# The last score block of a head pair as a step of its own, one MLP piece behind, in a fused attention and mixer kernel

## The chip, the core and the metric

The kernel runs on one core of one Trainium2 chip. The metric is the device time of one execution in microseconds (us), lower is better. Before the change it is 579.77 us, the median of 3 runs (577.92 to 579.84).

A core has the engines PE (matrix products, written into PSUM), ACT (activation functions), DVE and POOL (elementwise work and reductions), and SP, which here only issues DMA transfers. PEld is PE's loading of weights, beside its matmuls. PSUM has 8 banks for each partition, each of 512 fp32 columns.

## The reference

Attention with RMS-normalised queries and keys, then a mixer block on its output:

```python
q: (8 batches, 12 heads, 448 tokens, 64)      # k and v alike
q_n, k_n = rmsnorm(q, g_q), rmsnorm(k, g_k)
attn = softmax(q_n @ k_n.T / sqrt(64))
x = (attn @ v), heads side by side            # (8, 448, 768)
u = x + (x.T @ U @ V).T                       # U (448, 32), V (32, 448): along the tokens
out = u + relu(u @ w_ch1) @ w_ch2             # w_ch1 (768, 3072), w_ch2 (3072, 768)
```

## The kernel before

**Pieces of work.** For each batch the MLP is cut into 24 *up* pieces (`up`, L681: six matmuls of 448 columns into one PSUM tile `ph`, then one relu on ACT) and 24 or 32 *down* pieces (`down`, L728: six matmuls of 384 columns). Four down pieces in a row add into one PSUM tile `po`, which is allocated at part 0 and read by DVE (L738) after part 3. Between them stand the mixer's steps `mix_t` and `mix_two` for the next batch, whose results go through DMA transposes into `uT`.

Attention goes by pairs of heads, six pairs to a batch, two to a group (24 groups of four heads). The 448 keys of a pair of heads are three blocks of 128 for each head and a last stretch of 64 for each; the two stretches of 64 form one block together, the *last block*. In the loop `Spair` (from group 6 on) scores one pair: two blocks into two one-bank tiles `sl` (L455), their exponentials (ACT, L457), four blocks into two tiles `sc` of two banks each (L464), the last block into a third `sl` (L466), its exponential (L467), and the two exponentials of the `sc` tiles (L469). `Vall` (L529, L533) multiplies the exponentials of the pair before with the values.

The last 64 queries of a group are worked apart: `rest_tile` allocates a tile `pr`, `rest_products` (L560) fills it for both pairs of the group before, `rest_norms` (DVE) divides it into `x_rest` (the tile that traces call `xr`). `Spair` gets that group's number as `rest` where it does this work first: at the first pair of a group, except where a separate step `Rest` does it (first pair of batches 2 and 3). `Srows` is the form of the step in batch 1.

**PSUM.** The pool `ps_sc` has two buffers of two banks, the pool `ps` four of one bank. All of `ph`, `po`, `pv`, `pr`, `sl` and the mixer's small tiles come from `ps`; a new tile waits until the last reader of the buffer it gets is done.

**Order.** Instructions run in the order in which the program issues them on each engine. Batch 0's attention is written out by hand (`FRONT`). The rest is merged from two lists, `att` (attention steps with a cost) and `mlp` (MLP pieces with a cost). At each turn an attention step is taken if the sum of attention costs so far is at most `due` of the sum of MLP costs, and if `ready` allows it; otherwise an MLP piece is. `at` holds an estimate of when PE, ACT and DVE are done with what has been issued, and `runs` adds to it. `after_pair` is true from a `Spair` to the next MLP piece. If a mixer step comes next while it is true, a down piece from behind is moved ahead of it. An MLP piece of a batch whose attention is not complete waits (`done_at`, `may_mlp`).

**Other steps named below.** `squares`, `sums`, `roots` and `scale_all` prepare queries and keys of later groups (POOL L144, ACT L141, DVE L167, ACT L174 and L175, POOL L179, L198 and L202), `turn_dma` and `take_dma` turn them by DMA (L391, L393) and scale `qT` on POOL (L399), `load` fetches later groups, `weights` issues the loads of `w_ch1` and `w_ch2` from POOL's queue (L295, L303).

Of the kernel before, what the change touches and what calls it, by code (L numbers as in the profile page):

```python
# [12 lines left out]
AF = mybir.ActivationFunctionType  # L13
# [14 lines left out]
def kernel(  # L28
# [13 lines left out]
    nc = tc.nc  # L42
    B, H, S, D = q.shape
# [6 lines left out]
    NJ = S // P  # L50
    SM = NJ * P
    R = S - SM
# [7 lines left out]
    NPAIR = H // 2  # L60
    HALF = dm // 2
    scal = 1.0 / (D ** 0.5)
# [65 lines left out]
    def load(gi):  # L128
        stage_tiles(gi)
        for i in range(2):  # L130
            load_qk(gi, i)
        load_v(gi)
# [138 lines left out]
    bias = gg[:, 1:2]  # L271
# [79 lines left out]
    at = {"pe": 0.0, "act": 0.0, "dve": 0.0}  # L351
    exp_done = {}

    def runs(eng, us):
        at[eng] = us + (at["pe"] if eng == "pe" else max(at["pe"], at[eng]))

    qk, es, xs = {}, {}, {}
# [87 lines left out]
    def Spair(b, pr, rest=None):  # L445
        qT, kT = qk[divmod(b * NPAIR + pr, 2)]
        E = es[(b, pr)] = ep.tile([P, NB, S], BF16, name="E", tag="E")
        ts = [ps.tile([P, 512], FP32, name="sl", tag="ps")[:, :S] for _ in range(2)]
        if rest is not None:
            rest_tile(rest)  # L450
            rest_products(rest)
            rest_norms(rest)
        for i in range(2):
            d = slice(i * D, (i + 1) * D)
            nc.tensor.matmul(ts[i], kT[d, 2 * P:3 * P], qT[d], start=True, stop=True)  # L455
        for i in range(2):
            nc.scalar.activation(E[:, 4 + i, :], ts[i], AF.Exp, scale=scal, bias=bias)  # L457
        runs("pe", 0.4)
        runs("act", 1.04)
        tiles = [ps_sc.tile([P, 2, 512], FP32, name="sc", tag="sc") for _ in range(2)]  # L460
        for r in range(2):
            for i in range(2):
                d = slice(i * D, (i + 1) * D)
                nc.tensor.matmul(tiles[r][:, i, :S], kT[d, r * P:(r + 1) * P], qT[d], start=True, stop=True)  # L464
        last = ps.tile([P, 512], FP32, name="sl", tag="ps")[:, :S]
        nc.tensor.matmul(last, kT[:, SM:], qT, start=True, stop=True)  # L466
        nc.scalar.activation(E[:, 6, :], last, AF.Exp, scale=scal, bias=bias)  # L467
        for r in range(2):
            nc.scalar.activation(E[:, 2 * r:2 * r + 2, :], tiles[r][:, :, :S], AF.Exp, scale=scal, bias=bias)  # L469
        runs("pe", 0.6)  # L470
        runs("act", 2.3)
        exp_done[(b, pr)] = at["act"]

    def Srows(blocks, rest=None):
# [43 lines left out]
    x_rest = [consts.tile([P, dm], BF16, name=f"xr{i}") for i in range(2)]  # L518
# [48 lines left out]
    def rest_norms(gi):  # L567
        b, h0, _ = groups[gi]
        pv = rest_tiles.pop(gi)
        lo, hi = (0, R) if b % 2 else (R, P)  # L570
        r = headp.tile([P, 2], FP32, name="r", tag="r")
        nc.vector.reciprocal(r, pv[:, :, D])
        for e in range(2):
            rows = slice(e * R, (e + 1) * R)
            c = (h0 + 2 * e) * D
            nc.vector.tensor_tensor(
                x_rest[b % 2][lo:hi, c:c + 2 * D].rearrange("p (h d) -> p h d", d=D),
                pv[rows, :, :D],
                r[rows].rearrange("p h -> p h ()").to_broadcast([R, 2, D]), ALU.mult)
        runs("dve", 0.6)  # L580

    def rest_tile(gi):
        rest_tiles[gi] = ps.tile([P, 2, D1], FP32, name="pr", tag="ps")
# [168 lines left out]
    def add_att(cost, f, *a):  # L752
        att.append((cost, f, a))
# [15 lines left out]
    for i, (b, pr) in enumerate(pairs):  # L769
        if b == 0:  # L770
            continue
        gi, a = divmod(i, 2)
        more = gi + 1 < len(groups)
        by_dma = gi + 1 >= DMA_FROM
        soon = gi + 2 < len(groups)

        rest = gi - 1 if a == 0 and (pr > 0 or b > APART) else None
        if a == 0 and pr == 0 and b > 1:
            add_att(0.8, Vall, *pairs[i - 1])
            if gi == DMA_FROM:  # L780
                add_att(0.0, sums, gi + 1, 0)
                add_att(0.0, sums, gi + 1, 1)
                add_att(0.0, scale_all, gi + 1)
            if b <= APART:
                add_att(0.5, Rest, gi - 1)
        if gi >= DMA_FROM:
            add_att((0.5 if a == 1 and soon else 1.0) + (0.35 if rest is not None else 0.0), Spair, b, pr, rest)
            if a == 0 and more:
                add_att(0.0, turn_dma, gi + 1)
                add_att(0.0, take_dma, gi + 1)  # L790
                if gi + 3 < len(groups):
                    add_att(0.0, load, gi + 3)
            if pr != 0:
                add_att(0.5, Vall, *pairs[i - 1])
                if a == 1 and soon:
                    add_att(0.0, squares, gi + 2, 0)
                    add_att(0.0, squares, gi + 2, 1)
                add_att(0.25, lambda: None)
                if a == 1 and soon:
                    add_att(0.0, sums, gi + 2, 0)  # L800
                    add_att(0.0, sums, gi + 2, 1)
                    add_att(0.5, lambda: None)
                    add_att(0.0, scale_all, gi + 2)
            continue

        if a == 0:
            add_att(0.45, Srows, ((b, pr, 0), (b, pr, 1)), rest)
            if pr == 0:
                add_att(0.8, lambda: None)
            if not by_dma:  # L810
                add_att(0.0, squares, gi + 1, 0, nc.gpsimd)
                add_att(0.0, squares, gi + 1, 1, nc.gpsimd)
                if gi + 2 < DMA_FROM:
                    add_att(0.0, load, gi + 3)
            if pr != 0:
                add_att(0.9, Vall, *pairs[i - 1])
            add_att(0.0, sums, gi + 1, 0)
            add_att(0.0, sums, gi + 1, 1)
            add_att(1.0, Srows, ((b, pr, 2), (b, pr + 1, 0), (b, pr, 3)))
            add_att(0.0, scale_all, gi + 1)  # L820
            if gi + 2 == DMA_FROM:
                add_att(0.0, squares, gi + 2, 0, nc.gpsimd)
                add_att(0.0, squares, gi + 2, 1, nc.gpsimd)
                add_att(0.0, weights, 2)
            add_att(0.4, lambda: None)
        else:
            add_att(0.6, Srows, ((b, pr, 1), (b, pr, 2), (b, pr, 3)))
            if gi + 2 == DMA_FROM:
                add_att(0.0, load, gi + 3)
            if not by_dma:  # L830
                add_att(0.5, Vall, *pairs[i - 1])
                add_att(0.39, T, gi + 1, 0)
                add_att(0.39, T, gi + 1, 1)
                continue
            add_att(0.0, squares, gi + 2, 0)
            add_att(0.0, squares, gi + 2, 1)
            add_att(0.5, Vall, *pairs[i - 1])
            add_att(0.0, turn_dma, gi + 1)
            add_att(0.0, take_dma, gi + 1)
            add_att(0.0, load, gi + 3)  # L840
# [5 lines left out]
    for n, (c, f, a) in enumerate(att):  # L846
        gi = a[0] if f is Rest else a[2] if f is Spair else None
# [5 lines left out]
    mlp = []  # L853
    for b in range(B):
# [14 lines left out]
        tiles = [(col, half) for col in cols for half in range(2)]  # L869
        if b == 0:  # L870
            tiles.sort(key=lambda t: t[1])
        if b == B - 1:
            tiles = tiles[:-2]
# [68 lines left out]
    for step in FRONT.split():  # L942
# [4 lines left out]
            fill_mixer()  # L947
        if name == "val":
            load(int(a[0]) + 3)
    for i in range(2):  # L950
        nc.gpsimd.memset(x_rest[i][R:] if i else x_rest[i][:R], 0.0)
    weights(2)

    at.update(pe=0.0, act=0.0, dve=0.0)
# [27 lines left out]

    def ready(f, a):
        if f is Spair:
            if a[2] is not None and mlp[im][1] is down and mlp[im][2][3] > 0:
                return False
            if im > 0 and mixes(mlp[im - 1][1]):
                return False
            return at["dve"] <= at["pe"] + 0.3 and at["act"] <= at["pe"] + 0.6
        if f in (Vall, Rest) and ca >= a_one and (after_pair or after_v):  # L990
            return False
        if f is sums and a[0] > DMA_FROM:
            return not any(m[1] is mix_t for m in mlp[max(0, im - 1):im + 3])
        if ca >= a_one:
            return True
        if f is Vall:
            return exp_done[a[:2]] <= at["pe"] + 0.1
        return f is not Srows or at["act"] <= at["pe"] + 0.6

    later, turning, after_pair, after_v = [], False, False, False  # L1000
    while ia < len(att) or im < len(mlp):
# [6 lines left out]
        if take_att:  # L1008
            c, f, a = att[ia]
# [4 lines left out]
            after_pair = after_pair or f is Spair  # L1014
# [8 lines left out]
        else:  # L1023
            f = mlp[im][1]
# [4 lines left out]
            after_pair = after_v = False  # L1029
            c, f, a, _ = mlp[im]  # L1030
# [34 lines left out]
```

## Time and profile before

| | |
|---|---|
| runs shown | 579.84, 577.92, 579.77 us |
| the profiled execution | 579.34 us, of which 577.6 us are its span |
| granted PE clock | 1.0 |
| busy share of the span | PE 98%, ACT 53%, POOL 36%, DVE 33% |
| matmuls | 4762 |
| DMA | 68.20 MB, mean 118 GB/s |

Times in the rows are microseconds from the start of the span. A row of the timeline has start, length, engine, line of the kernel and operation, output and inputs by their names in the program, the count of instructions that the row holds together, and in brackets the idle time before it with what ended it. Rows of the same kind in close succession are merged, so that rows of one engine can overlap. Matmuls are pipelined and their ends are modelled: what PE's queue really spends on a matmul is the distance from its start to the next start.

### The profile page before, as it was taken

The page shows a single profiled execution, that of the slowest core. Times are in us where ns is not written, and L with a number is a line of the kernel's source. Part 1 is how long each engine was busy: PE and PEld are TensorE (multiplying, and loading weights), DVE is VectorE, ACT ScalarE, POOL GpSimd, SP SyncE. Part 2 cuts the span into 40 slices and gives each one's busy share as a digit, 9 for nine tenths or more (in the row PEclk, how much of TensorE's full clock was granted, in tenths as well). Part 3 has the DMA queues.
Part 4 walks back from the last instruction along what each step waited for, and adds up shares of the span by engine and source line. Part 5 has one row for each costly group of instructions (what it writes and reads, how often), then busy time and mean ns, then how long its engine had stood idle before and what let it go on. Part 6 is the DMA issues. An engine that isn't in the chain of part 4 may idle for free.

```text
span 577.6 us, 11577 instructions
## 1 busy us (share of the span) xinstructions
PE 564.9 (98%) x4762; PEld 323.2 (56%) x4762; DVE 191.2 (33%) x426; ACT 308.3 (53%) x516; POOL 206.2 (36%) x308
## 2 busy tenths in 40 slices
PE   8899999999999999999999999999999999999997
PEld 7665555555655555555555555555565555555565
DVE  6865655312343221621234321631123410410011
ACT  5977760788453876367654478258744344014300
POOL 6874793365313615334514523342531000000000
PEclk9999999999999999999999999999999999999999
DMA  9999999784436742497246735275212310220022
GB/s 226 180 245 238 251 234 207 140 204 84 120 76 159 177 111 39 93 206 184 39 121 100 193 100 131 59 186 147 34 35 57 75 30 0 69 62 0 1 56 55
DMA packets 104829, 68.20 MB, mean 118 GB/s; under 512 B 66632, under 2 KB 100936, under 8 KB 104776
## 3 DMA queue, kind: packets, MB, share of 16 engines
q1 hardware_dynamic: 95124, 57.83, 43.4%
q0 software_dynamic: 9408, 9.44, 9.8%
q8 instruction: 37, 0.61, 0.5%
q10 hardware_dynamic: 244, 0.20, 0.1%
q14 instruction: 16, 0.13, 0.1%
HBM read 52.20 MB, written 11.01 MB: 109 GB/s over the span
## 4 chain that ended last, share of the span: by engine, by line
PE 80%; DMA 9%; ACT 3%; POOL 3%; issue 3%; SPq 0%; DVE 0%; POOLq 0%; ACTq 0%
PE po L728 34%; PE ph L681 33%; DMA kf<-in_k_dram 6%; PE pv L533 3%; DMA w2b<-in_moe_w_ch_dram 3%; PE sl L455 2%; ACT E L457 2%; POOL sq L144 2%; ACT E L435 1%; PE sl L466 1%; PE po L715 1%; PE sc L464 1%; PE pr L560 1%; PE pv L529 1%; PE sc L614 1%
## 5 line engine op out<-in xcount | busy, mean ns | idle before, releaser
L681 PE MATMUL ph<-uT,w1b 128*128 128x448 bf16 x1128 | 223.1, 352 | 1.1 <-DMA uT<-u_rest 0.7
L728 PE MATMUL po<-w2b,hT 128*128 128x384 bf16 x1296 | 221.9, 326 | 1.1 <-DMA w2b<-in_moe_w_ch_dram 1.0
L728 PEld LDWEIGHTS <-hT 128*128 128x128 bf16 x1296 | 123.5, 98 | 84.8 <-issue 7.1
L681 PEld LDWEIGHTS <-w1b 128*128 128x128 bf16 x1128 | 108.5, 98 | 98.7 <-issue 3.8
L688 ACT ACTIVATE hT<-ph 128x448 bf16<-128x448 f32 x186 | 98.3, 550 | 110.1 <-PE ph L681 109.7
L457 ACT ACTIVATE E<-sl,gg 128x448 bf16<-128x448 f32 x72 | 41.6, 630 | 79.2 <-PE sl L455 78.1
L399 POOL TENSOR_SCALAR qT<-qT,gg 128x448 bf16<-128x448 bf16 x36 | 50.5, 1402 | 92.2 <-DMA qT<-qn 80.7
L198 POOL TENSOR_TENSOR qn<-qf,rs 128x384 bf16<-128x384 f32 x36 | 29.9, 829 | 116.6 <-ACT rs L175 109.8
L469 ACT ACTIVATE E<-sc,gg 128x896 bf16<-128x896 f32 x72 | 68.9, 1020 | 0.0
L738 DVE TENSOR_TENSOR ob<-po,x 128x384 f32<-128x384 f32 x46 | 25.6, 557 | 108.9 <-PE po L728 104.9
L167 DVE TENSOR_REDUCE ssq<-sq 128x14 f32<-128x896 f32 x45 | 47.1, 1079 | 27.6 <-ACT sq L141 25.0
L537 DVE RECIPROCAL r<-pv 128x6 f32<-128x6 f32 x42 | 8.2, 195 | 124.2 <-PE pv L533 123.9
L435 ACT ACTIVATE E<-sc,gg 128x896 bf16<-128x896 f32 (+1 forms) x42 | 37.0, 952 | 2.2 <-PE sc L430 2.0
L533 PE MATMUL pv<-va,E 128*128 128x65 bf16 x756 | 35.4, 194 | 0.0
L533 PEld LDWEIGHTS <-E 128*128 128x128 bf16 x756 | 32.4, 98 | 3.4
L198 POOL TENSOR_TENSOR kp<-kf,rs 128x384 bf16<-128x384 f32 x36 | 29.8, 828 | 0.0
L529 PE MATMUL pv<-vl,E 128*128 128x130 bf16 x126 | 27.6, 219 | 0.0
L621 DVE TENSOR_TENSOR x<-sc,x 128x384 bf16<-128x384 f32 x42 | 20.8, 550 | 17.6 <-PE sc L614 17.6
L174 ACT ACTIVATE rs<-ssq,eps 128x28 f32<-128x28 f32 (+1 forms) x24 | 7.5, 314 | 35.6 <-DVE ssq L167 35.5
L538 DVE TENSOR_TENSOR x<-pv,r 128x384 bf16<-128x384 f32 x42 | 23.4, 557 | 1.4
L467 ACT ACTIVATE E<-sl,gg 128x448 bf16<-128x448 f32 x36 | 22.9, 637 | 0.0
L206 POOL CAST va<-vf 128x768 bf16<-128x768 f32 x24 | 20.7, 861 | 1.2 <-DMA vf<-in_v_dram 1.2
(123 smaller groups left out, 429.9 us busy)
## 6 DMA issues: line engine op xcount, KB each, us to landing
qf<-in_q_dram SPq DMA_DIRECT2D x23, 448.0 KB, 3.8
kf<-in_k_dram SPq DMA_DIRECT2D x23, 448.0 KB, 5.2
vf<-in_v_dram SPq DMA_DIRECT2D x48, 192.0 KB, 6.0
out_dram<-ob SPq DMA_DIRECT2D x48, 192.0 KB, 2.7
w2b<-in_moe_w_ch_dram POOLq DMA_DIRECT2D x8, 576.0 KB, 16.8
w1b<-in_moe_w_ch_dram POOLq DMA_DIRECT2D x2, 1152.0 KB, 19.2
vf<-in_v_dram SPq DMA_DIRECT2D x48, 32.0 KB, 5.2
w1b<-in_moe_w_ch_dram POOLq DMA_DIRECT2D x1, 1536.0 KB, 29.4
```

Source lines behind the costliest of these rows:

```text
L167: nc.vector.tensor_reduce(ssqs[gi][:, i, :], sqs.pop((gi, i)), AX, ALU.add)
L198: nc.gpsimd.tensor_tensor(main.rearrange("p (t i) d -> p i t d", i=2), src[:, c, :2 * NJ].rearrange("p (i t) d -> p i t d", i=2), rs[:, c, ...
L399: nc.gpsimd.tensor_scalar(qT[:, a], qT[:, a], gg[:, 0:1], None, ALU.mult)
L435: nc.scalar.activation(es[(b, pr)][:, 2 * r:2 * r + n, :], sc[:, :n, :S], AF.Exp, scale=scal, bias=bias)
L457: nc.scalar.activation(E[:, 4 + i, :], ts[i], AF.Exp, scale=scal, bias=bias)
L469: nc.scalar.activation(E[:, 2 * r:2 * r + 2, :], tiles[r][:, :, :S], AF.Exp, scale=scal, bias=bias)
L529: nc.tensor.matmul(pv[:, i].rearrange("p e d -> p (e d)"), E[:, 2 * NJ, w:w + P], vl[:, lp, :], start=True, stop=False)
L533: nc.tensor.matmul(pv[:, i, e, :], E[:, 2 * j + e, w:w + P], va[:, (lp + 2 * e) * NJ + j, :], start=False, stop=(e == 1 and j == NJ - 1))
L681: nc.tensor.matmul(ph, w1b[:, dt, ht * P:(ht + 1) * P], uT[:, dt, off:off + S], start=(dt == 0), stop=(dt == KD - 1))
L688: nc.scalar.activation(hT[:, ht, off:off + S], ph, AF.Relu)
L728: nc.tensor.matmul(po, hT[:, ht, col:col + P], w2b[:, ht, half * HALF:(half + 1) * HALF], start=(ht == 0), stop=(ht == KH - 1))
L738: nc.vector.tensor_tensor(ob[:, h], po, urows(b, col, half), ALU.add)
```

## The change

In a pair that carries a rest, `Spair` no longer scores the last block. A step `Slast` behind it does: its matmul and its exponential. `ready` holds `Slast` back until an MLP piece has been taken since the pair. The cost of the step, 1.35 with the rest, is charged at `Slast` instead of at `Spair`. In pairs without a rest `Spair` calls `Slast` itself, in the old place. The condition that kept a pair with a rest from being taken while a down product is open (next MLP piece a `down` with a part over 0) is dropped.

In `ready`, an `Srows` that carries a rest is now also held back while DVE's estimate is more than 0.9 ahead of PE's.

The two memsets of `x_rest` on POOL move from the end of the written-out part, ahead of two weight loads, into the list of attention steps, behind the squares for group 4 in group 3.

```diff
--- before.py
+++ after.py
@@ -462,13 +462,21 @@
             for i in range(2):
                 d = slice(i * D, (i + 1) * D)
                 nc.tensor.matmul(tiles[r][:, i, :S], kT[d, r * P:(r + 1) * P], qT[d], start=True, stop=True)
+        if rest is None:
+            Slast(b, pr)
+        for r in range(2):
+            nc.scalar.activation(E[:, 2 * r:2 * r + 2, :], tiles[r][:, :, :S], AF.Exp, scale=scal, bias=bias)
+        runs("pe", 0.4)
+        runs("act", 1.78)
+        exp_done[(b, pr)] = at["act"]
+
+    def Slast(b, pr):
+        qT, kT = qk[divmod(b * NPAIR + pr, 2)]
         last = ps.tile([P, 512], FP32, name="sl", tag="ps")[:, :S]
         nc.tensor.matmul(last, kT[:, SM:], qT, start=True, stop=True)
-        nc.scalar.activation(E[:, 6, :], last, AF.Exp, scale=scal, bias=bias)
-        for r in range(2):
-            nc.scalar.activation(E[:, 2 * r:2 * r + 2, :], tiles[r][:, :, :S], AF.Exp, scale=scal, bias=bias)
-        runs("pe", 0.6)
-        runs("act", 2.3)
+        nc.scalar.activation(es[(b, pr)][:, 2 * NJ, :], last, AF.Exp, scale=scal, bias=bias)
+        runs("pe", 0.2)
+        runs("act", 0.52)
         exp_done[(b, pr)] = at["act"]
 
     def Srows(blocks, rest=None):
@@ -579,6 +587,10 @@
                 r[rows].rearrange("p h -> p h ()").to_broadcast([R, 2, D]), ALU.mult)
         runs("dve", 0.6)
 
+    def fill_rest():
+        for i in range(2):
+            nc.gpsimd.memset(x_rest[i][R:] if i else x_rest[i][:R], 0.0)
+
     def rest_tile(gi):
         rest_tiles[gi] = ps.tile([P, 2, D1], FP32, name="pr", tag="ps")
 
@@ -784,7 +796,9 @@
             if b <= APART:
                 add_att(0.5, Rest, gi - 1)
         if gi >= DMA_FROM:
-            add_att((0.5 if a == 1 and soon else 1.0) + (0.35 if rest is not None else 0.0), Spair, b, pr, rest)
+            add_att(0.0 if rest is not None else 0.5 if a == 1 and soon else 1.0, Spair, b, pr, rest)
+            if rest is not None:
+                add_att(1.35, Slast, b, pr)
             if a == 0 and more:
                 add_att(0.0, turn_dma, gi + 1)
                 add_att(0.0, take_dma, gi + 1)
@@ -810,6 +824,8 @@
             if not by_dma:
                 add_att(0.0, squares, gi + 1, 0, nc.gpsimd)
                 add_att(0.0, squares, gi + 1, 1, nc.gpsimd)
+                if gi == 3:
+                    add_att(0.0, fill_rest)
                 if gi + 2 < DMA_FROM:
                     add_att(0.0, load, gi + 3)
             if pr != 0:
@@ -947,8 +963,6 @@
             fill_mixer()
         if name == "val":
             load(int(a[0]) + 3)
-    for i in range(2):
-        nc.gpsimd.memset(x_rest[i][R:] if i else x_rest[i][:R], 0.0)
     weights(2)
 
     at.update(pe=0.0, act=0.0, dve=0.0)
@@ -982,11 +996,11 @@
 
     def ready(f, a):
         if f is Spair:
-            if a[2] is not None and mlp[im][1] is down and mlp[im][2][3] > 0:
-                return False
             if im > 0 and mixes(mlp[im - 1][1]):
                 return False
             return at["dve"] <= at["pe"] + 0.3 and at["act"] <= at["pe"] + 0.6
+        if f is Slast:
+            return not after_pair
         if f in (Vall, Rest) and ca >= a_one and (after_pair or after_v):
             return False
         if f is sums and a[0] > DMA_FROM:
@@ -995,7 +1009,7 @@
             return True
         if f is Vall:
             return exp_done[a[:2]] <= at["pe"] + 0.1
-        return f is not Srows or at["act"] <= at["pe"] + 0.6
+        return f is not Srows or at["act"] <= at["pe"] + 0.6 and (len(a) == 1 or a[1] is None or at["dve"] <= at["pe"] + 0.9)
 
     later, turning, after_pair, after_v = [], False, False, False
     while ia < len(att) or im < len(mlp):
```

## The prediction

> **What bounds the kernel now.** I read the page first (busy time, clock, groups), then the waits of PE, then the chain that ended last, then the timeline around the pairs that the change touches. From the page, parts 1, 2 and 5:
>
> ```profile
> span 577.6 us, 11577 instructions
> PE 564.9 (98%) x4762; PEld 323.2 (56%) x4762; DVE 191.2 (33%) x426; ACT 308.3 (53%) x516; POOL 206.2 (36%) x308
> PEclk9999999999999999999999999999999999999999
> L681 PE MATMUL ph<-uT,w1b 128*128 128x448 bf16 x1128 | 223.1, 352 | 1.1 <-DMA uT<-u_rest 0.7
> L728 PE MATMUL po<-w2b,hT 128*128 128x384 bf16 x1296 | 221.9, 326 | 1.1 <-DMA w2b<-in_moe_w_ch_dram 1.0
> ```
>
> PE is busy from end to end at full granted clock, and the two MLP products have next to no idle time before them. ACT at 53% and POOL at 36% have room. So the program is one long queue on PE, and an edit is worth what it takes out of, or puts into, the places where that queue stops. The change removes no matmul. The waits name the stops (us in total, times, longest; the first two from the answer for PE alone, the third from that for all engines):
>
> ```profile
> PE sl L466 <- ACT E L457: 2.1, 6, 0.4
> PE po L728 <- DMA w2b<-in_moe_w_ch_dram: 1.0, 1, 1.0
> PEld L430 <- DVE kT L383: 0.8, 3, 0.4
> ```
>
> L466 is the matmul of the last score block; it waits six times for the first exponential of its own pair (L457). The chain that ended last runs through L457 more often than six times: 16 steps, of which the first and the last are
>
> ```profile
> 116.70 0.63 ACT E L457
> 449.82 0.64 ACT E L457
> ```
>
> Sixteen is also the number of pairs from group 7 on that carry a rest: the even pair of groups 7, 8, 10, 11 and 12 to 23. So all 16 hold PE up, though only six show as idle. Matmul ends are modelled, so a shorter stop can only be seen from start to start.
>
> **The change, part by part.** (1) The last block becomes a step behind one MLP piece. Three stretches of the timeline price it. First, a pair with a rest taken while a down product is open:
>
> ```profile
> 300.95 0.36 PE L455 MATMUL sl<-qT,kT 64*128 64x448 bf16 x2
> 301.15 0.54 PE L464 MATMUL sc<-qT,kT 64*128 64x448 bf16 x4
> 301.35 1.16 ACT L457 ACTIVATE E<-sl,gg 128x448 bf16<-128x448 f32 x2 [0.66 <-PE sl L455]
> 302.03 0.35 PE L466 MATMUL sl<-qT,kT 128*128 128x448 bf16 x1 [0.34 <-ACT E L457]
> 302.22 3.09 PE L728 MATMUL po<-w2b,hT 128*128 128x384 bf16 x18
> ```
>
> Second, a pair with a rest between two up pieces (the rows of the answer for this stretch that matter):
>
> ```profile
> 323.34 0.54 ACT L688 ACTIVATE hT<-ph 128x448 bf16<-128x448 f32 x1 [1.82 <-PE ph L681]
> 323.41 0.26 PE L560 MATMUL pr<-va,E 128*64 128x65 bf16 x6
> 323.61 0.36 PE L455 MATMUL sl<-qT,kT 64*128 64x448 bf16 x2
> 323.81 0.54 PE L464 MATMUL sc<-qT,kT 64*128 64x448 bf16 x4
> 324.01 1.16 ACT L457 ACTIVATE E<-sl,gg 128x448 bf16<-128x448 f32 x2
> 324.28 0.36 PE L466 MATMUL sl<-qT,kT 128*128 128x448 bf16 x1
> 324.69 3.57 PE L681 MATMUL ph<-uT,w1b 128*128 128x448 bf16 x18
> 325.05 0.64 ACT L467 ACTIVATE E<-sl,gg 128x448 bf16<-128x448 f32 x1
> 325.57 1.92 ACT L469 ACTIVATE E<-sc,gg 128x896 bf16<-128x896 f32 x2
> 327.35 1.49 ACT L688 ACTIVATE hT<-ph 128x448 bf16<-128x448 f32 x3
> 328.09 0.22 PE L529 MATMUL pv<-vl,E 128*128 128x130 bf16 x1
> ```
>
> Third, a pair without a rest:
>
> ```profile
> 332.53 0.54 PE L464 MATMUL sc<-qT,kT 64*128 64x448 bf16 x4
> 333.01 0.36 PE L466 MATMUL sl<-qT,kT 128*128 128x448 bf16 x1
> 333.21 2.06 PE L681 MATMUL ph<-uT,w1b 128*128 128x448 bf16 x10
> ```
>
> The third is the undisturbed pace: 0.48 us from the first of the four `sc` matmuls to the last block, 0.20 from there to the MLP. In the first the step to the last block takes 302.03 - 301.15 = 0.88, so 0.88 - 0.47 = 0.41 more than in the second. In the second that step is undisturbed (324.28 - 323.81 = 0.47), but the next takes 324.69 - 324.28 = 0.41 against 0.20: 0.21 more. In both, PE moves about 0.1 us after the first of the two exponentials at L457 has ended (301.35 + half of 1.16 = 301.93; 324.01 + 0.58 = 324.59).
>
> The reason is the pool `ps` with four buffers. A pair with a rest takes four at once: two `sl`, `pr`, the last `sl`. If a down piece holds one open, the last `sl` is the fifth and waits for the first `sl`; if none is open, the next MLP tile is the fifth and waits for the same. A pair without a rest takes three and never waits. After the change the rest pair takes three, an MLP piece runs, and the last block comes when the first `sl` has long been read. What of the new order could be late next? Without an open product, the next MLP tile takes the buffer of the piece before; its relu ended at 323.34 + 0.54 = 323.88, before 324.28, where that tile would now start. With one open, the piece asks for no buffer. The last block comes a piece of some 1.1 us after 324.28, when the first `sl` has been free since 324.59. The ring then returns to the first up piece's buffer at the fourth request behind it: 324.28 + three pieces of (328.09 - 324.69) / 3 = 1.13 + 0.20 = 327.88. ACT, which now does the four `sc` blocks from 325.05 and then the relu, ends that at 325.05 + 1.92 + 0.50 = 327.47. That leaves 0.4 us, and I count no new wait. The product that needs the moved block comes only after the next pair's scores, at 332.53 or later, so the later exponential has cover.
>
> Sum of (1): the waits give six stops of the first kind, the chain leaves ten of the second: 6 x 0.41 + 10 x 0.21 = 2.46 + 2.10 = 4.56 us gained.
>
> Against it stands the price of a lone matmul between MLP pieces. The nearest row is a mixer matmul of 384 columns that stands alone so:
>
> ```profile
> 45.89 0.33 PE L669 MATMUL pm<-x,Vr 128*128 128x384 bf16 x1
> 46.05 2.43 PE L681 MATMUL ph<-uT,w1b 128*128 128x448 bf16 x12
> ```
>
> It holds the queue for 46.05 - 45.89 = 0.16 us, although its own record lasts 0.33. By that the lone last block costs its 0.20 again, as inside the pair: nothing added. The upper bound is its whole record, 0.36 - 0.20 = 0.16 more for each of 16, 2.6 us; I take nothing, because the row is of the same tile shape between the same pieces. The Trainium skill, page "TensorE: Matmul & The Clock Gate", section "Single matmul latency", gives a matmul that cannot hide its drain (398 + N) / 2.4 ns warm, for N = 448 an estimated 353 ns; read as the cost of every lone step, that would take 2.4 us off the gain. The rows above do not bear this reading out here: 0.16 us, not 0.33.
>
> (2) Pairs may now be taken inside an open down product. Following the planner's due times by hand, about four of the 16 come two to nine pieces earlier; they had one of the two stops and lose it in either place. Cost zero. The transposes, the POOL scaling of `qT` and the loads listed behind the pair keep their due place, since the 1.35 is charged to the last block one piece later; they prepare the following group, a dozen us ahead.
>
> (3) The new condition on `Srows` lets DVE finish `kT` first. From the answer for PE alone:
>
> ```profile
> 73.34 0.26 PE L560 MATMUL pr<-va,E 128*64 128x65 bf16 x6
> 73.68 0.55 PE L430 MATMUL sc<-qT,kT 64*128 64x448 bf16 x4
> ```
>
> The step is 0.34 here and 0.20 where the scores do not wait (323.41 to 323.61), so 0.14, in two places (the other near 60 us): 0.28 gained. Both steps are put off by one up piece (one of them by a mixer step too) and stand directly ahead of the value product that follows anyway, so nothing later moves.
>
> (4) The memsets. From the answer for POOL:
>
> ```profile
> 35.93 1.52 POOL L951 MEMSET xr<- 64x768 bf16 x2
> 37.40 1.71 POOL L303 DMA_DIRECT2D w2b<-in_moe_w_ch_dram  x2
> 48.30 1.68 POOL L144 TENSOR_TENSOR sq<-kf 128x896 f32<-128x896 f32 x1 [1.52 <-DMA kf<-in_k_dram]
> 55.13 1.69 POOL L179 TENSOR_TENSOR qn<-qf,rs 128x896 bf16<-128x896 f32 x1 [5.15 <-ACT rs L175]
> 78.14 1.70 POOL L303 DMA_DIRECT2D w2b<-in_moe_w_ch_dram  x2
> ```
>
> They move from 35.93 to behind the squares at 48.30, into the 5.15 us in which POOL waits for ACT: 49.98 + 1.52 = 51.5, hidden. Without that cover POOL's later steps, the weight issue at 78.14 among them, would be 1.5 us later. The first two weight transfers start 1.5 us sooner. PE's one stop for weights (1.0 us in the waits) is on the last transfer, issued at 78.14, whose own issue POOL's later waits decide. Bounds: that stop goes (-1.0) or grows by the lost cover (+1.5). I take 0.
>
> Together 4.56 + 0.28 = 4.84. The profiled execution took 579.34 us (577.6 of span and 1.7 around it), 0.43 under the median of the runs shown; 574.5 for it, so 575.0 as a median.
>
> **The rivals.** *Only the open products gain*: if the buffers are handed out in another order, so that the first MLP tile still asks for the first `sl`, the ten small stops stay: 2.46 + 0.28 gained, 577.0. Both kinds of stop end with the same exponential, which speaks for a plain ring and against this.
>
> *A lone matmul pays its record*: 2.6 us of the gain go, 577.6. The L669 row is against it.
>
> *Nothing changes*: if the last block lands directly behind its pair (the planner takes it at once where the MLP may not go on), or an equal stop arises elsewhere: 579.8. Such a place exists at one pair of the 16 at most.
>
> *ACT becomes the bound, slower*: the relu of the piece behind a pair now stands ahead of a ring with 0.4 us to spare. The price is the lateness beyond 0.4 us at each of the ten pairs. With one square ahead of the exponentials,
>
> ```profile
> 83.70 0.96 ACT L141 ACTIVATE sq<-qf 128x896 f32<-128x896 f32 x1
> ```
>
> it is 10 x 0.56 = 5.6 and 580.6; with two, 10 x 1.5 = 15 and 590. It makes the kernel slower by over 0.5% from a lateness of 1.2 us on. For it: ACT has four exponentials, a relu and the last one in a row. Against it: the exponentials start 0.40 us after the first score matmul (323.61 to 324.01), so ACT is not late at such a pair today, and the squares are queued behind the other pair of each group.
>
> **How the numbers follow.** Forecast 0.72, only the open products 0.08, lone matmul 0.05, nothing changes 0.06, ACT late 0.09. What a measurement can tell from no change is about 0.5%, 2.9 us, so faster means under 576.9. The forecast is faster; the second case lies at the border, and I give it half: 0.76 faster, 0.15 same, 0.09 slower. The low end is the forecast with the weight stop gone and 0.8 for the spread of the runs (577.92 to 579.84): 573.2. The high end takes in the two partial cases: 578.0. The likeliest case's own range is 573.2 to 576.6.
>
> **What would show it.** Right: no wait of the last block's matmul for L457; about 0.2 us from that matmul to the next in all 36 pairs; 0.47 from the four `sc` matmuls to the MLP piece; the memset rows between 50 and 52 us; span near 573. Wrong: a wait of an up tile or of `pv` for the relu behind a pair, a longer stop at the last `w2b`, or rows of the last block directly behind the `sc` rows in pairs with a rest.

## The result, and the profile after

| comparison | before, median | after, median | ratio, 95% interval |
|---|---|---|---|
| the one that was predicted | 579.75 us (5 runs, 576.45 to 579.84) | 572.18 us (5 runs, 571.75 to 572.83) | 0.9887 [0.9859, 0.9915] |
| repeated on a second chip | 578.35 us (23 runs) | 572.06 us (6 runs, 571.48 to 574.78) | 0.9904 [0.9874, 0.9934] |
| repeated on a third chip | 578.72 us (11 runs) | 573.73 us (6 runs, 572.57 to 574.86) | 0.9926 [0.9906, 0.9946] |

The kernel became faster, by 7.6, 6.3 and 5.0 us. The forecast was a gain of 4.84, with 575.0 us as the time and 573.2 as the low end of the range; the measured 572.18 lies below that range. What follows is mostly about the 2.7 us between the first of these gains and the sum.

The profiled execution after took 571.75 us (570.0 of span) at a granted clock of 1.0. From its page:

```profile
span 570.0 us, 11579 instructions
PE 562.8 (99%) x4762; PEld 323.4 (57%) x4762; DVE 191.4 (34%) x425; ACT 308.7 (54%) x517; POOL 206.3 (36%) x308
PE 96%; ACT 2%; DVE 1%; issue 0%; POOL 0%; POOLq 0%
L693 PE MATMUL ph<-uT,w1b 128*128 128x448 bf16 x1128 | 223.9, 352 | 0.0
L740 PE MATMUL po<-w2b,hT 128*128 128x384 bf16 x1296 | 223.5, 326 | 0.0
```

The third line is the chain that ended last. Before, the same line of the page read:

```profile
PE 80%; DMA 9%; ACT 3%; POOL 3%; issue 3%; SPq 0%; DVE 0%; POOLq 0%; ACTq 0%
```

The matmuls are the same 4762, and both MLP groups have lost all the idle time that stood before them. But the chain has also lost DMA, POOL and issue, 15 points of the span together, which the prediction had not counted on. (A share of the chain is not a gain in time: it says what the end of the program hung on.) The whole answer for the waits of PE after:

```profile
PE busy L245 <- POOL ident masks.py:199: 1.4, 1, 1.4
PE sc L430 <- ACT E L435: 1.0, 5, 0.2
PE pt L368 <- DVE kp L179: 0.8, 1, 0.8
PE pv L500 <- ACT E L435: 0.2, 1, 0.2
```

The last score block's matmul (now L476) no longer waits for the exponential at L457; that was expected. The stops for the last `w2b` (1.0) and for `uT` (0.7) are gone as well; neither is in the sum. The rows of the timeline around one pair with a rest, those that matter:

```profile
315.98 0.36 PE L455 MATMUL sl<-qT,kT 64*128 64x448 bf16 x2
316.17 0.54 PE L464 MATMUL sc<-qT,kT 64*128 64x448 bf16 x4
316.37 1.16 ACT L457 ACTIVATE E<-sl,gg 128x448 bf16<-128x448 f32 x2 [0.38 <-PE sl L455]
316.65 1.15 PE L740 MATMUL po<-w2b,hT 128*128 128x384 bf16 x6
317.63 0.35 PE L476 MATMUL sl<-qT,kT 128*128 128x448 bf16 x1
317.82 4.51 PE L693 MATMUL ph<-uT,w1b 128*128 128x448 bf16 x23
319.20 0.65 ACT L477 ACTIVATE E<-sl,gg 128x448 bf16<-128x448 f32 x1
```

From the four `sc` matmuls to the MLP piece 316.65 - 316.17 = 0.48, the piece 0.98, the lone last block 0.19. The two exponentials of L457 end at 317.53, and the block comes behind the first of them without a wait. In this profile the step from the last block to the next matmul is about 0.20 in all 36 pairs; before, it was 0.41 in ten of them.

**Four stretches.** To see where the time went I cut the span at four landmarks: the first up matmul, the first down matmul, the first up matmul of batch 1, and the first matmul of the last 72 down products. From the timelines of PE, first before, then after:

```profile
41.54 1.30 PE L681 MATMUL ph<-uT,w1b 128*128 128x448 bf16 x6
77.96 3.09 PE L728 MATMUL po<-w2b,hT 128*128 128x384 bf16 x18
110.15 5.08 PE L681 MATMUL ph<-uT,w1b 128*128 128x448 bf16 x26 [0.71 <-DMA uT<-u_rest]
566.10 8.02 PE L715 MATMUL po<-w2b,hT 128*128 128x384 bf16 x72
```

```profile
40.78 1.30 PE L693 MATMUL ph<-uT,w1b 128*128 128x448 bf16 x6
76.91 3.09 PE L740 MATMUL po<-w2b,hT 128*128 128x384 bf16 x18
107.03 5.84 PE L693 MATMUL ph<-uT,w1b 128*128 128x448 bf16 x30
558.54 8.02 PE L727 MATMUL po<-w2b,hT 128*128 128x384 bf16 x72
```

| stretch | before | after | gained | in the sum |
|---|---|---|---|---|
| start to first up (the front) | 41.54 | 40.78 | 0.76 | 0 |
| to the first down (holds `Srows`) | 36.42 | 36.13 | 0.29 | 0.28 |
| to batch 1's first up (holds the stops for `w2b`, `uT`) | 32.19 | 30.12 | 2.07 | 0 |
| to the last 72 (holds the 16 pairs) | 455.95 | 451.51 | 4.44 | 4.56 |
| together | 566.10 | 558.54 | 7.56 | 4.84 |

So the two terms of the sum are there within 0.12 and 0.01 us, and 2.83 us more came from stretches in which the change does nothing but move the memsets. One theory was that the moved memsets brought this: the first weight transfers start sooner, the later ones land in time, both stops go. The rival was that these stretches differ from one execution to the next whatever the kernel, and that the profile of before had caught a late one.

### The profile page after: what moved, and what is told of

Same layout as the page of the kernel before. It is cut to its first block, busy times and chain, and to the rows that moved or that the text cites. A ratio compares the mean times of both kernels' runs of the same rounds, so it can differ in the third digit from the quotient of the medians.

```text
span 570.0 us, 11579 instructions
## 1 busy us (share of the span) xinstructions
PE 562.8 (99%) x4762; PEld 323.4 (57%) x4762; DVE 191.4 (34%) x425; ACT 308.7 (54%) x517; POOL 206.3 (36%) x308
## 4 chain that ended last, share of the span: by engine, by line
PE 96%; ACT 2%; DVE 1%; issue 0%; POOL 0%; POOLq 0%
PE po L740 38%; PE ph L693 37%; PE pv L541 4%; PE sc L464 2%; PE sl L455 2%; ACT E L435 2%; PE busy L245 2%; PE sl L476 2%; PE pr L568 1%; PE po L727 1%; PE pv L537 1%; PE sc L430 1%; PE sc L711 1%; PE sc L626 1%; PE pt L368 1%; PE pu L609 1%
## 5 line engine op out<-in xcount | busy, mean ns | idle before, releaser
L700 ACT ACTIVATE hT<-ph 128x448 bf16<-128x448 f32 x187 | 99.7, 550 | 106.9 <-PE ph L693 106.5
L457 ACT ACTIVATE E<-sl,gg 128x448 bf16<-128x448 f32 x72 | 41.6, 630 | 76.1 <-PE sl L455 75.3
L750 DVE TENSOR_TENSOR ob<-po,u_rest 128x384 f32<-128x384 f32 x8 | 4.5, 558 | 47.9 <-PE po L740 47.7
```

Source lines behind the costliest of these rows:

```text
L700: nc.scalar.activation(hT[:, ht, off:off + S], ph, AF.Relu)
L750: nc.vector.tensor_tensor(ob[:, h], po, urows(b, col, half), ALU.add)
```

## The experiments

**The parts one by one, on one chip** (before beside them 579.41 us, 23 runs, 576.42 to 580.91). *step_only* is the kernel after with the memsets in their old place and the old condition on `Srows`; *memset_back* has only the memsets in the old place; *memset_only* and *srows_only* are the kernel before with that one part:

```diff
 # memset_only: the kernel before, with
-    for i in range(2):
-        nc.gpsimd.memset(x_rest[i][R:] if i else x_rest[i][:R], 0.0)
     weights(2)
...
+                if gi == 3:
+                    add_att(0.0, fill_rest)
 # srows_only: the kernel before, with
-        return f is not Srows or at["act"] <= at["pe"] + 0.6
+        return f is not Srows or at["act"] <= at["pe"] + 0.6 and (len(a) == 1 or a[1] is None or at["dve"] <= at["pe"] + 0.9)
```

> The changed kernel with the memsets in their old place and without the new condition on Srows: only the last block as its own step and pairs inside open down products. Theory 1 (the 2.8 us more than forecast are PE's stops for the last weight transfer, 1.0 us idle, and for uT, 0.7 us idle, at 97 and 110 us, and it is the memsets' place that takes them away): 4.6 us under the kernel before, 575.2, the waits of PE still show w2b and uT. Theory 2 (those stops come and go with the start of each execution, whatever the edit): 575 in the mean, the stops in some executions and not in others. Theory 3 (the step itself takes more than 4.6 us): 572 to 573.

> The kernel before with only the two memsets moved behind the squares for group 4. Theory 1: the stops at w2b and uT are gone, about 2 us under the kernel before, 577.7. Theory 2: the same as the kernel before within 0.5 us, with its spread of 3 us from run to run. Theory 3: the same as the kernel before. The recorded price of the edit was nothing, with bounds of -1.0 and +1.5.

> The kernel before with only the new condition on Srows. All theories: 0.3 us under the kernel before; the step from the rest products to the scores at 60 and 73 us falls from 0.34 to 0.20 us.

> The changed kernel with only the memsets back in their old place, ahead of the first two w2b loads. Theory 1: the stops at w2b and uT are back, about 2 us over the changed kernel, 574.2. Theory 2 and 3: the same as the changed kernel, 572.2.

| kernel | median, us | ratio, 95% interval |
|---|---|---|
| step_only | 574.58 (6 runs) | 0.9918 [0.9887, 0.9949] |
| memset_only | 579.09 (12 runs) | 0.9994 [0.9977, 1.0012] |
| srows_only | 578.86 (12 runs) | 0.9990 [0.9972, 1.0007] |
| memset_back | 575.07 (6 runs) | 0.9925 [0.9900, 0.9949] |

The step alone carries the gain that was forecast for it. Moving the memsets alone brings nothing that the times show: its interval ends at 0.9977, that is at 1.3 us, and excludes a gain of 2.07 in every execution, but not a gain of up to 1.3 in the mean. *memset_back* missed the 572.2 of the second and third theory and came near the 574.2 of the first: 575.07, with 32.05 in its third stretch. That is 2.9 us over the 572.18 of the kernel after, which did not run on this chip. The 0.28 of `Srows` is too small for a comparison of times, but the timeline of srows_only has it: 36.14 from first up to first down. The step from the rest products to the scores fell from 0.34 to 0.19 in both places; the first of them:

```profile
61.64 0.26 PE L560 MATMUL pr<-va,E 128*64 128x65 bf16 x6
61.83 0.55 PE L430 MATMUL sc<-qT,kT 64*128 64x448 bf16 x4
```

With the memsets in the old place, the waits of PE in the profile of step_only name both stops:

```profile
PE po L740 <- DMA w2b<-in_moe_w_ch_dram: 0.8, 1, 0.8
PE ph L693 <- DMA uT<-u_rest: 0.7, 1, 0.7
```

In the profile of memset_only they are missing, and the six stops at the last block are there:

```profile
PE sl L466 <- ACT E L457: 2.1, 6, 0.4
```

That looked like the first theory, against the times. But the front of that execution was late: its first up matmul started at 45.00 us, 3.5 later than before's 41.54, so that PE asked for everything later.

**The order of two issues, the piece between, the place, and the kernel after once more, on a second chip** (before 578.35, 23 runs). *swap* is the kernel before with the memsets kept where they are but behind the weight issues: the first weights start sooner, and nothing else moves. *no_piece* is the kernel after with `Slast` allowed at once. *veto* is the kernel after with the old condition against open down products put back.

```diff
 # swap: the kernel before, with
+    weights(2)
     for i in range(2):
         nc.gpsimd.memset(x_rest[i][R:] if i else x_rest[i][:R], 0.0)
-    weights(2)
 # no_piece: the kernel after, with
         if f is Slast:
-            return not after_pair
+            return True
 # veto: the kernel after, with, in ready for Spair,
+            if a[2] is not None and mlp[im][1] is down and mlp[im][2][3] > 0:
+                return False
```

> The changed kernel itself once more, on one chip with the three kernels below. From the first four profiles: the stretch from batch 1's first up piece to the last matmul is 463.76 us with the old pairs and 459.32 with the step (4.44 less), from the first up piece to the first down piece 36.42 or 36.14 (0.28 less with the new condition on Srows), from the first down piece to batch 1's first up piece 30.12 with the memsets moved and 31.5 to 32.2 without; the front before the first up piece took 40.8 to 45.0. Theory 1 (the moved memsets take the w2b and uT stops away in every execution): 4.44 + 0.28 + 2.06 = 6.8 under the kernel before, all runs. Theory 2 (those stops only show when the front was quick; a slow front hides them, so the time of many executions is set by the loads of the start and not by the memsets): about 5 us under the kernel before in the mean, with a spread of 3 to 4 us, and the five tight first runs were quick fronts.

> The kernel before with the two memsets directly behind the two w2b loads instead of ahead of them: the loads are issued 1.5 us sooner, POOL's work is otherwise in the old order. Theory 1 (the sooner issue of the first two w2b loads is what counts, the software queue works in order): 30.1 us from the first down piece to batch 1's first up piece, and the same time as with the memsets moved away (579.1 there, 0.3 under before; 2 under by the stretch alone). Theory 3 (it is POOL's free time, the preparation of group 3 that then starts sooner): 32 us in that stretch, as before.

> The changed kernel, but the last block's step may be taken at once, so that it follows its pair without an MLP piece between. If the piece between is what saves, the stops for the first exponential are back: 16 pairs, 9 or 10 of them now inside an open down product, 10 x 0.41 + 6 x 0.21 = 5.4 us over the changed kernel. If the separate step or the exponentials' new order is what saves: the same as the changed kernel.

> The changed kernel with the old condition put back that a pair with a rest isn't taken inside an open down product. By the forecast's step 2 the place of a pair costs nothing: the same as the changed kernel within 0.3 us, 459.3 us from batch 1's first up piece to the last matmul. Rival: the freed place is worth something of its own, up to 0.2 us at each of the four pairs that move.

| kernel | median, us | ratio, 95% interval | fourth stretch |
|---|---|---|---|
| after_again | 572.06 (6 runs) | 0.9904 [0.9874, 0.9934] | 451.51 |
| swap | 578.54 (12 runs) | 0.9997 [0.9975, 1.0019] | as before |
| no_piece | 577.94 (12 runs) | 1.0002 [0.9983, 1.0021] | 456.56 |
| veto | 573.54 (6 runs) | 0.9922 [0.9895, 0.9949] | 451.48 |

*after_again* does not decide between its theories: 6.3 us under before, with an interval from 3.8 to 7.3, where one expected 6.8 and the other about 5. Its profile has slow loads at the start (1.25 MB between 4 and 8 us, see below), a late front of 43.80 and no stop: 30.12 in the third stretch.

*no_piece* is the clearest. The last block is a step of its own, but directly behind its pair, and the whole gain of the step is gone: 456.56 against 451.51. Its two landmarks:

```profile
107.78 5.84 PE L693 MATMUL ph<-uT,w1b 128*128 128x448 bf16 x30
564.34 8.02 PE L727 MATMUL po<-w2b,hT 128*128 128x384 bf16 x72
```

The waits of PE have the old stop back, nine times:

```profile
PE sl L476 <- ACT E L457: 3.1, 9, 0.4
```

Its timeline shows one of them, with an open down product, rows that matter:

```profile
319.52 0.54 PE L464 MATMUL sc<-qT,kT 64*128 64x448 bf16 x4
320.41 0.35 PE L476 MATMUL sl<-qT,kT 128*128 128x448 bf16 x1 [0.34 <-ACT E L457]
320.60 1.14 PE L740 MATMUL po<-w2b,hT 128*128 128x384 bf16 x6
```

That is 0.89 from the `sc` matmuls to the block, against 0.88 in such a pair before. Nine instead of six, since the condition against open products is dropped here: by the prediction's prices 9 x 0.41 + 7 x 0.21 = 5.16, measured 456.56 - 451.51 = 5.05. So the piece between is the cure. That the four buffers of the pool `ps` are the cause is argued from the program and from the instruction that ends the wait, the reader of the first `sl`; no run has another number of buffers. *veto* takes four of the 16 pairs at another place than the kernel after and shows that the freed place is worth nothing: 451.48 and 451.51 are the same.

*swap* starts the first `w2b` issue ahead of the memsets and changes nothing that the times show (a gain of up to 1.4 us is not excluded); the stops are smaller in its profile, not gone, and its third stretch is 31.62, nearer the 32 of the third theory than the 30.1 of the first:

```profile
PE ph L681 <- DMA uT<-u_rest: 0.6, 1, 0.6
PE po L728 <- DMA w2b<-in_moe_w_ch_dram: 0.6, 1, 0.6
```

And with the memsets moved, the profile of *veto* still has the stop for `uT`:

```profile
PE ph L693 <- DMA uT<-u_rest: 0.4, 1, 0.4
```

**The kernel before, unchanged, twice, and memset_only twice.** If the execution decides, then an unchanged kernel must show executions with the stops and others without them.

> The kernel before once more, for its profile: how the time up to the first up piece (the front) and the stops for w2b and uT go together from one execution to the next. If a late front hides the stops (theory 2): the front and the stretch from the first down piece to batch 1's first up piece add up to about 73 to 74 us whatever the front. If they are apart (theory 1): 32 us in that stretch for any front.

> The kernel before, a third execution with a profile: as for the first look.

> The kernel before with only the memsets moved, once more, for its profile. Theory 1: 30.1 us from the first down piece to batch 1's first up piece at any front. Theory 2: 30.1 us only where the front is late (43 us and more) or the loads are quick; with a front near 41.5 and slow loads up to 32.

> The kernel before with only the memsets moved, a third execution with a profile: as for the first look.

The unchanged kernel took 576.89 and 580.84 us, memset_only 577.11 and 576.32. The first of the unchanged executions has no stop at all in the third stretch; its landmarks:

```profile
41.07 1.30 PE L681 MATMUL ph<-uT,w1b 128*128 128x448 bf16 x6
77.49 3.09 PE L728 MATMUL po<-w2b,hT 128*128 128x384 bf16 x18
107.61 5.84 PE L681 MATMUL ph<-uT,w1b 128*128 128x448 bf16 x30
563.57 8.02 PE L715 MATMUL po<-w2b,hT 128*128 128x384 bf16 x72
```

The third stretch is 107.61 - 77.49 = 30.12, the same as after. One thing that differs from the profile that I had predicted from is how fast the first loads came. The DMA view of the same 4 us at the start (4 to 8 us), long before the first instruction that the change touches: before as predicted from, before_look1, before_look2, and after.

```profile
DMA packets 729, 1.23 MB, mean 306 GB/s; under 512 B 45, under 2 KB 729, under 8 KB 729
```

```profile
DMA packets 845, 1.42 MB, mean 354 GB/s; under 512 B 55, under 2 KB 845, under 8 KB 845
```

```profile
DMA packets 728, 1.23 MB, mean 307 GB/s; under 512 B 43, under 2 KB 728, under 8 KB 728
```

```profile
DMA packets 823, 1.38 MB, mean 345 GB/s; under 512 B 53, under 2 KB 823, under 8 KB 823
```

So the two profiles of the first comparison were of executions of different kinds: loads of 1.23 MB before, of 1.38 MB after. Set against the quick execution of the unchanged kernel, the change is worth 563.57 - 558.54 = 5.03 us at the last landmark: 4.45 in the fourth stretch, 0 in the third, 0.29 in the second and 0.29 in the front (576.89 - 571.75 = 5.14 as times).

**The memsets once more, in the kernel after, on one chip** (before 578.72, 11 runs). *after_third* is the kernel after, *memset_back_again* the same with the memsets in the old place.

> The changed kernel a third time. Fourteen profiles so far fall into two kinds by what the loads move between 4 and 8 us: 1.33 MB and more (quick) or 1.25 MB and less (slow), before any changed instruction runs. Quick executions have no stop for w2b, whichever kernel; slow ones with the memsets in the old place have one. With like kinds the change is worth 4.7 to 5.1 us. So a quick execution should take 571.5 to 572.8 and a slow one 574 to 575. Theory A (the kind is drawn anew in each execution, alike for all kernels): about one run in four is quick, as with the kernel before, median 574. Theory B (something in the changed kernel makes quick loads more frequent): three in four quick again, median 572.

> The changed kernel with the memsets in the old place, a second time. Quick executions 571.5 to 573, slow ones with the two stops 574.5 to 576.5. Theory A: the same share of quick runs as the changed kernel beside it. Theory B with the memsets as its cause: one run in six quick, as in the first comparison, and the changed kernel beside it mostly quick.

After_third 573.73 us (0.9926 [0.9906, 0.9946]), memset_back_again 573.30 us (0.9919 [0.9895, 0.9944]), six runs each. No difference between the two, and the 2.9 us between memset_back and the kernel after do not come back; that speaks for theory A. The profiled execution of after_third had slow loads (1.16 MB) and yet took 572.96 us, where 574 to 575 was expected of such a one. The profile of memset_back_again has no stop in the third stretch although its loads were slow (1.20 MB in 4 to 8 us) and its memsets stand in the old place; its front was late, and PE came late enough:

```profile
43.40 1.30 PE L693 MATMUL ph<-uT,w1b 128*128 128x448 bf16 x6
79.54 3.09 PE L740 MATMUL po<-w2b,hT 128*128 128x384 bf16 x18
109.65 5.65 PE L693 MATMUL ph<-uT,w1b 128*128 128x448 bf16 x29
```

79.54 to 109.65 is 30.11. Over all 16 profiles: the third stretch is 31.5 to 32.2 in six of the eight with the memsets in the old place (*swap* counted here), and 30.1 in the two others (quick loads, or a late front; a late front doesn't always do it, before_look2 has 43.34 and 31.87); with the memsets moved it is 30.1 to 30.3 in seven of eight and 30.7 in *veto*. Five of those eight had quick loads and two of the others a front at 43.8 and 45.0, so what the memsets add to this can't be read from the profiles. In the times they add nothing that three comparisons found (memset_only, swap, and this pair).

One row of POOL separates the profiles better than the loads do, the first issue of `w2b`. In *swap*, which has a stop at `w2b`, and in *after_again*, which has none:

```profile
35.49 1.70 POOL L303 DMA_DIRECT2D w2b<-in_moe_w_ch_dram  x2
34.63 1.71 POOL L303 DMA_DIRECT2D w2b<-in_moe_w_ch_dram  x2
```

In the six profiles with a stop at `w2b` this row starts between 35.49 and 39.20 us, in the ten without one between 31.83 and 35.24. The memsets ahead of it are 1.5 us of that; the executions differ by more, since POOL came to this place anywhere from 31.83 to 37.73 us. Why it came so early or so late is not shown.

## Why the prediction was right, and where it failed

**(1) The last block, 4.56 forecast: right.** 4.4 to 4.5 less in the fourth stretch of every profile that has the step behind a piece. The six stops and the ten small ones behind them were real, and *no_piece* brings them back. The rival by which only the open products gain would have left 2.10 of it behind.

**The lone matmul, priced at its 0.20 again: right.** 317.63 to 317.82 is 0.19. The rule of the Trainium skill (page "TensorE: Matmul & The Clock Gate", section "Single matmul latency") that I set beside it would have taken 2.4 us off; the trace does not bear that reading out.

**ACT as the bound, slower: did not happen.** No up tile and no `pv` waits for a relu in the waits after.

**(2) The freed place, 0: right**, by *veto*. **(3) `Srows`, 0.28: right**, 0.28 to 0.29 less in the second stretch of every profile with that condition.

**(4) The memsets, 0, and the low end: here it failed.** The value 0 stands as far as the times show (a mean gain of up to 1.3 us is not excluded): the memsets went into POOL's pause. Their rows in the timeline of POOL after:

```profile
45.34 1.68 POOL L144 TENSOR_TENSOR sq<-kf 128x896 f32<-128x896 f32 x1 [2.77 <-DMA kf<-in_k_dram]
46.95 1.52 POOL L592 MEMSET xr<- 64x768 bf16 x2
```

That is earlier than the 50 to 52 that I gave, since the squares ahead of them came earlier in that execution (45.34 instead of 48.30). What failed is the step that treated PE's stops outside the pairs as belonging to the kernel. I took one profile, found 1.0 us for the last `w2b` in it, put it into the low end as a bound of the memsets, and left the 0.7 for `uT` out altogether. The runs show that both stops and the front change with the execution: the unchanged kernel has one with the stops and 43.34 of front, and one without them and 41.07. The profile that the sum was made against was a late one (32.19 in the third stretch, 41.54 of front), the one after an early one (30.12 and 40.78); 2.07 + 0.76 = 2.83 us of difference that no part of the change had to earn. With the 0.7 of the second stop, which one profile did show, the low end would have been 572.5, still 0.3 over the measured 572.18; the front's 0.76 could only be seen in a second profile of the same kernel.

**What the change is worth** is therefore the 4.7 us of the like-for-like stretches (4.44 + 0.28), and 5.0 between the quick executions. The repeats on two other chips gave 6.3 and 5.0, and 4.72 of 579 is a ratio of 0.9918: inside both their intervals, just outside that of the first comparison (up to 0.9915). The other four runs that have the step behind a piece lie at 4.3 to 5.4 us under the before beside them (step_only, memset_back, veto, memset_back_again). So a part of the 7.6 us of the first comparison was luck with the executions.

**What stays open.** Why the five executions of the kernel after in the first comparison all came out within 571.75 to 572.83, while four of before's five took 577.92 or more. Loads are known of the profiled ones alone; they differ before any changed instruction runs, so the runs here offer no mechanism. All five had a granted clock of 1.0, which 23 of the 58 runs of before beside the experiments had not (last section); for the five runs of before in that comparison the clock is not on record. And whether the moved memsets help an execution with slow loads and an early front: after_third is the one such profile with moved memsets (1.16 MB, front 41.85), and its third stretch is 30.25, against 31.5 to 32.2 in such executions with the memsets in the old place. One profile is not enough to call it shown, and it isn't a like one: its POOL issued the first `w2b` at 33.20, sooner than POOL even came to the memsets in those others (35.49 to 36.23).

## What to carry to other kernels

When PE is full, count the buffers that a step asks for at once against those that its pool has: a request too many is a stop for the first reader, whose price can be read from start to start even where the waits show none, and one other piece of work between the requests removes it. Take a stop that hangs on a transfer as belonging to one execution until a second profile of the same kernel shows it again; take such stops out of the comparison by cutting both timelines at the same landmarks. A gain larger than the sum of its parts is a reason to repeat the comparison on another chip, not to look for one more part.

## What the runs showed of the hardware that was not expected

**The loads of one kernel differ from execution to execution.** Between 4 and 8 us the loads moved 1.16 to 1.43 MB in the 16 profiles here, in two groups (up to 1.26 and from 1.33), and the time of the unchanged kernel ran from 576.1 to 580.9 us.

**The granted clock can halve in the front.** Some executions have a mean granted clock of 0.993 to 0.997 instead of 1.0: of the 58 runs of before beside the experiments, 23 did, and they took 578.97 to 580.91 us, while the 22 at 1.0 have a median of 577.80 (the other 13 had 0.999). In memset_only's profiled execution it can be seen in a table of stretches (window, its length, PE busy and matmuls, granted clock, DMA share, GB/s):

```profile
21.00:22.40 1.40, 0.02 (x1) 1.00 0.15 35
22.40:24.40 2.00, 1.73 (x24) 0.97 0.52 152
24.40:25.40 1.00, 0.09 (x2) 0.50 1.07 173
25.40:27.00 1.60, 1.60 (x11) 0.50 1.05 180
```

PE stood almost still for 1.4 us, worked for 2.0, and ran at half clock from about 24.4 on; its first up matmul started at 45.00, against 41.37 in another execution of the same kernel with quicker loads (moved_look1) and 41.85 in after_third, whose loads were as slow (1.16 MB) and whose clock was 1.0. The Trainium skill, page "TensorE: Matmul & The Clock Gate", section "What's actually happening", has the half rate follow an idle window of about 3.4 us. The half rate is in this trace; an idle window of that length is not: ahead of the half rate stand a pause of 1.4 us and 2.0 us with 1.73 us of work, and the pause of 0.9 us behind them falls in the half rate already.
